# Attention with a routed feed-forward: values loaded once and repeated on GpSimd, and products grouped by the columns they use

## Chip, core and metric

The kernel runs on one core of a Trainium2 chip. The metric is device time in microseconds (us). The core has five engines: TensorE (PE, with its weight loads shown as PEld), VectorE (DVE), ScalarE (ACT), GpSimd (POOL) and SyncE (SP, which issues most transfers). Each executes its own instructions in the order in which the program lists them; an instruction that waits holds everything behind it on its engine.

## The reference

Eight batches of eight heads, 576 positions, 64 numbers a head. Four heads attend to the last 32 positions, four to every fourth of the last 128 (the "dilated" heads). The result, 4608 rows of 512, goes through a mixture of experts: noisy gating picks two of eight experts for each row.

```python
scores = scale * np.matmul(q, k.transpose(0, 1, 3, 2))
mask_plain = (rel >= 0) & (rel < window)                                        # window 32
mask_dil = (rel >= 0) & (rel < window * dilation) & (rel % dilation == 0)       # dilation 4
attn = softmax(scores where masked)
x = (attn @ v) as rows of 512
noisy_logits = x @ w_gate + log1p(exp(x @ w_noise)) * noise
for e in range(E):                                                              # top two experts of a row
    h = np.maximum(x[mask] @ w1[e], 0.0)
    out[mask] += top2_w[mask, k, None] * (h @ w2[e])
```

## The kernel before, in words

**Attention** works through 8 groups of 3 steps. Group g holds two batches and one kind of head: even groups the dilated heads, odd groups the plain ones. K and Q of a kind stand in one buffer (`KT`, `QT`), V of the dilated heads in `VD`, of the plain heads in two tiles `VP`. Loads for later groups are entered in a table of slots (`at(slot, f)`), two slots a step, and are issued by SP when the program comes to the slot.

A step is: mask products (`identb` times a mask, all 128 output columns), 24 score products that use 32 columns each (`qk`), a maximum and a subtraction on DVE, an exponential on ACT (`expo`), six 128-column transposes of the result (`ptr`), copies to SBUF on ACT, 24 value products of 32 columns (`pv`), and a division on DVE. The result `x` of an older step is stored to DRAM, transposed (`x_transpose`, 128 columns), and multiplied with the gating weights (`gate_mm`, 32 columns); `gate_front` transposes three pieces of the logits in half of the steps. Step i of the loop issues, in this order, the scores of step i, the transposes of step i-1, the slot's fillers, the transposes of x of step i-2, the exponential of step i, the values of step i-1 and the gating product of step i-2.

In one value product the 128 rows of V are 64 own positions and the 64 before and between them: for a block of 64 positions, the windows need three pieces of 32 positions, and the middle one twice. The array `vdl` (`vpl`) in DRAM holds 128 rows of such windows, so that each position is loaded twice. V has a second axis `w`; rows of the other `w` are zero and are cleared once at the start, on ACT for `VD`, on DVE and POOL for `VP`.

**Setup**: POOL and DVE build masks and constants. `setup_a`, `setup_b` and `setup_c` are fillers of the slots 2, 4 and 5. `setup_b` writes an index table `tokc` on POOL and computes on it on DVE; `setup_c` prepares rows of padding, some of it in slots 6, 12 and 18.

**Gating and routing** (`gate`) runs in small pieces between the attention steps (`micro`). Its scatters to the table `tab` are indirect DMAs on POOL; a copy from the newest `x` to a one-element tile `spacer` holds POOL back so that only some of them are issued in a step. The first expert's rows are gathered by indirect DMAs on POOL as well.

**Experts**: eight experts, three blocks of rows each, products `up` and `dn` on TensorE, which is in order, so that the first of them stands behind the last piece of attention.

Of the kernel before, what the change touches and what calls it, by code (L numbers as in the profile page):

```python
# [9 lines left out]
F32 = mybir.dt.float32  # L10
# [15 lines left out]
U = 4  # L26
# [14 lines left out]
US_W2 = 3.0, 3.5  # L41
LAG = 15
US_X = (17, 52)


@with_exitstack
def attention_moe_kernel(ctx, tc, qt, kp, kd, vpl, vdl, w_gate, w_noise, noise, w1, w2, out, CAPS=(1216, 1216, 1216, 1184, 1184, 1152, 1152, 1152), SPLITS=(0, 384, 896)):
# [65 lines left out]
    def v_loads(g):  # L113
        u, ty = g // 2, 1 - g % 2
        if ty:
            d = VD.rearrange("p w j h y c -> p w (j h y c)")
            n = d.shape[2] // 3
            for i in range(3):
                for w in range(2):
                    yield lambda i=i, w=w: sync.dma_start(d[w:128:2, w, n * i:n * i + n],  # L120
                                                          vdl[u, w:128:2, n * i:n * i + n])
        else:
            for b in range(2):
                for w in range(2):
                    yield lambda b=b, w=w: sync.dma_start(VP[b][w:128:2, w].rearrange("p j h c -> p (j h c)"),
                                                          vpl[u, b, w:128:2])
# [7 lines left out]
    gpsimd.memset(KT[1][:, 1], 0.0)  # L134
    for f in qk_loads(0, 2):
        f()

    def clear_by_copy(t):
        scalar.copy(t, none.to_broadcast(list(t.shape)) if len(t.shape) == 2 else
                    none.unsqueeze(2).unsqueeze(3).to_broadcast(list(t.shape)))  # L140

    VF = VD.rearrange("p w j h y c -> p w (j h y c)")
    for w in range(2):
        clear_by_copy(VF[:, w])
    clear_by_copy(KT[0][:, 0])


# [45 lines left out]
            p0 = 64 * x + 32 * h  # L193
            gpsimd.tensor_copy(m[p0:p0 + 32, 6 * h], m0[p0:p0 + 32, 1])
    vector.memset(KT[0][:, 1], 0.0)
    for b, w, eng in ((0, 0, vector), (0, 1, gpsimd), (1, 0, gpsimd), (1, 1, gpsimd)):
        eng.memset(VP[b][:, w], 0.0)
# [153 lines left out]

    SB, PE_, PT, XG, XT, GS = {}, {}, {}, {}, {}, {}

    def qk(k):
        g, st = divmod(k, 3)
        ty = 1 - g % 2
        s = aps.tile([128, 8, 2, 64], F32, name="s", tag="s")
        for e in (0, 4):
            n = min(4, 6 - e)
            tensor.matmul(s[:, e:e + n], lhsT=identb,  # L360
                          rhs=masks[ty][:, 6 * st + e:6 * st + e + n].unsqueeze(2).to_broadcast([128, n, 2, 64]),
                          start=True, stop=False, skip_group_check=True)
        for e in range(6):
            for qd in range(4):
                if ty == 0:
                    x = qd // 2
                    b, ub = divmod(12 * st + 6 * (qd % 2) + e, 18)
                else:
                    x = qd
                    b, ub = divmod(6 * st + e, 9)  # L370
                tensor.matmul(s[32 * qd:32 * qd + 32, e], lhsT=QV[ty][:, b, x, 32 * ub:32 * ub + 32],  # L371
                              rhs=KV[ty][:, :, b, x, 32 * ub:32 * ub + 64],
                              start=False, stop=True, skip_group_check=True)
        a = sm.tile([128, 2, 6, 64], F32, name="a", bufs=1)
        mx = sm.tile([128, 6, 2], F32, name="mx")
        vector.tensor_reduce(mx, s[:, 0:6], axis=AX.X, op=OP.max)
        vector.tensor_tensor(a.rearrange("p y e c -> p e y c"), s[:, 0:6], mx.unsqueeze(3).to_broadcast([128, 6, 2, 64]), op=OP.subtract)
        SB[k] = a

    def expo(k):  # L380
        p = sm.tile([128, 6, 64, 2], F32, name="pe")
        scalar.activation(p.rearrange("p j c w -> p j w c"), SB.pop(k).rearrange("p y (j w) c -> p (y j) w c", w=2),
                          AF.Exp, scale=0.125)
        PE_[k] = p

# [14 lines left out]
    def pv(k):  # L400
# [510 lines left out]
    def at(kb, *fs):  # L911
        fill.setdefault(kb, []).extend(fs)
# [3 lines left out]
    for g in range(2 * U):  # L916
        s0 = 6 * g
        if g + 1 < 2 * U:
            for i, f in enumerate(v_loads(g + 1)):
                at(s0 + 3 + 2 * (i // 2), f)  # L920
# [3 lines left out]
    fronts = {6 * u + 6 + st: (u, st) for u in range(U) for st in range(3)}  # L924
    def idx_late(before, a, b, then):
        while any(g in gens for g in before):
            yield 1
# [36 lines left out]
    for t0, n, kb in ((0, 9, 17), (9, 9, 29), (18, 6, 39), (24, 3, 41), (27, 6, 51)):  # L964
        at(kb, lambda t0=t0, n=n: gens.append(gate(t0, n)))
    L0 = 12 * (U - 1)
    at(29, lambda: (new_idx(0), gens.append(idx_late(list(gens), 0, SPLITS[1], lambda: x_block(0)))))
    at(41, lambda: gens.append(idx_late(list(gens), SPLITS[1], SPLITS[2], lambda: x_block(1))))
    at(2, setup_a)
    at(4, setup_b)  # L970
    at(5, setup_c)
    for f in v_loads(0):
        f()
    for f in qk_loads(1):
        f()

# [31 lines left out]
    for i in range(NS + 2):  # L1008
        slot[0] = 2 * i
        early[0] = True  # L1010
        micro(2)
        early[0] = False
        if i < NS:
            qk(i)
        micro(2)
        if i >= 2:
            move_x(i - 2)
        micro(2)
        if 1 <= i <= NS:
            ptr(i - 1)  # L1020
        micro(2)
        micro(2)
# [7 lines left out]
        micro(2)  # L1030
        if 1 <= i <= NS:
            pv(i - 1)
        micro(2)
# [8 lines left out]
    for f in fronts.values():  # L1042
        gate_front(*f)
    gens.append(gate(33, 3))

# [137 lines left out]
def _layouts(q, k, v):  # L1183
# [10 lines left out]
    def windows(a):  # L1194

        n = a.shape[1] // 64
        a = np.pad(a, ((0, 0), (32, 0)) + ((0, 0),) * (a.ndim - 2))
        p = np.arange(128)[:, None]
        at = 64 * np.arange(n) + p // 2 + 32 * (p % 2)
        return a[:, at]  # L1200

    qt = np.stack([heads(q, ty).reshape(U, 128, 4 * S) for ty in range(2)], 1)
    pad = ((0, 0),) * 4 + ((32, 0),)
# [2 lines left out]
    def with_ones(a):  # L1206
        return np.concatenate([a, np.ones(a.shape[:-1] + (1,), np.float32)], -1)

    vpl = windows(with_ones(v[:, 0:4].transpose(0, 2, 1, 3))).reshape(U, 2, 128, -1)

    dil = v[:, 4:8].reshape(U, 2, 4, S // 4, 2, 2, D).transpose(0, 1, 4, 3, 2, 5, 6).reshape(U, S, 4, 2, D)
    vdl = windows(with_ones(dil)).reshape(U, 128, -1)
    return {"qt": qt, "kp": kp, "kd": kd, "vpl": vpl, "vdl": vdl}


# [18 lines left out]
```

## Time and profile before

| | |
|---|---|
| median of 3 runs | 1081.24 us (1080.13 to 1085.15) |
| span of the profiled execution | 1086.8 us |
| granted TensorE clock, mean | 0.963 |
| PE busy | 1011.7 us (93%) |
| PEld / DVE / ACT / POOL busy | 79% / 43% / 29% / 49% |
| first mask product, step 0 | 9.6 us |
| first mask product, step 23 | 197.6 us |
| first expert product | 227.2 us |

The profiled execution is 5.6 us longer than the median, and 1.7 us longer than the longest run. A row of the timeline gives the start, the time, engine and line, output and inputs, and in brackets how long the engine had been idle and what ended that. A busy PE is not a PE at its peak. PE is above 97% busy from 400 us to the end, so that the first 227 us, where the change lies, are to be read apart from the whole.

### The profile page before, as it was taken

The page shows a single profiled execution, that of the slowest core. Times are in us where ns is not written, and L with a number is a line of the kernel's source. Part 1 is how long each engine was busy: PE and PEld are TensorE (multiplying, and loading weights), DVE is VectorE, ACT ScalarE, POOL GpSimd, SP SyncE. Part 2 cuts the span into 40 slices and gives each one's busy share as a digit, 9 for nine tenths or more (in the row PEclk, how much of TensorE's full clock was granted, in tenths as well). Part 3 has the DMA queues.
Part 4 walks back from the last instruction along what each step waited for, and adds up shares of the span by engine and source line. Part 5 has one row for each costly group of instructions (what it writes and reads, how often), then busy time and mean ns, then how long its engine had stood idle before and what let it go on. Part 6 is the DMA issues. An engine that isn't in the chain of part 4 may idle for free. (4 is left out here: it accounts for less than half of the span.)

```text
span 1086.8 us, 18768 instructions
## 1 busy us (share of the span) xinstructions
PE 1011.7 (93%) x7274; PEld 855.7 (79%) x7275; DVE 465.7 (43%) x1060; ACT 319.4 (29%) x609; POOL 534.5 (49%) x727
## 2 busy tenths in 40 slices
PE   6896877778989999999999999999999999999996
PEld 4774655567878989988997889788978888888885
DVE  7673635635225444344434352435353434343221
ACT  6673534622113322222223131312131222222110
POOL 7004243455776655755644564466455645553112
PEclk9998887878999999999999999999999999999999
DMA  8898687455255243533533352426242623453123
GB/s 280 313 315 278 194 283 257 151 164 186 43 96 129 54 109 85 109 84 86 91 85 85 86 131 50 102 64 135 38 112 52 137 39 108 75 119 72 24 28 45
DMA packets 79214, 132.95 MB, mean 122 GB/s; under 512 B 31648, under 2 KB 41296, under 8 KB 77840
## 3 DMA queue, kind: packets, MB, share of 16 engines
q1 hardware_dynamic: 56768, 92.56, 27.6%
q0 software_dynamic: 22352, 39.15, 19.6%
q8 instruction: 58, 0.95, 0.4%
q14 instruction: 36, 0.29, 0.1%
HBM read 92.11 MB, written 39.54 MB: 121 GB/s over the span
## 5 line engine op out<-in xcount | busy, mean ns | idle before, releaser
L826 PE MATMUL up<-x,w1h 128*128 128x512 f32 (+4 forms) x1536 | 396.7, 344 | 10.9 <-issue 8.2
L778 POOL DMA_INDIRECT g<-xs,ixi x258 | 269.7, 1045 | 84.0 <-issue 78.6
L826 PEld LDWEIGHTS up<-x,w1h 128*128 128x128 f32 x1536 | 273.1, 189 | 37.2 <-issue 8.7
L826 PE MATMUL up<-x,w1l 128*128 128x384 f32 (+4 forms) x768 | 263.4, 343 | 0.0
L868 PE MATMUL dn<-w2h,hh 128*128 128x512 f32 x576 | 225.5, 392 | 0.0
L868 PE MATMUL dn<-w2l,hh 128*128 128x512 f32 x576 | 224.7, 390 | 0.0
L868 PE MATMUL dn<-w2h,hl 128*128 128x512 f32 x576 | 224.6, 390 | 0.0
L832 DVE SCALAR_TENSOR_TENSOR hl<-up,hh 128x384 fp32r<-128x384 f32 (+2 forms) x192 | 106.7, 557 | 249.1 <-ACT hh L830 187.0
L830 ACT ACTIVATE hh<-up 128x384 fp32r<-128x384 f32 (+4 forms) x192 | 94.6, 498 | 298.7 <-PE up L826 248.7
L845 POOL DMA_INDIRECT out_rows<-y,ixs x67 | 107.3, 1602 | 141.4 <-DVE y L877 119.0
L826 PEld LDWEIGHTS up<-x,w1l 128*128 128x128 f32 x768 | 145.4, 189 | 11.8
L877 DVE TENSOR_SCALAR y<-dn,ixs 128x512 f32<-128x512 f32 x63 | 47.3, 751 | 188.2 <-PE dn L868 163.5
L868 PEld LDWEIGHTS dn<-w2h,hl 128*128 128x128 f32 x576 | 108.4, 188 | 22.7
L868 PEld LDWEIGHTS dn<-w2h,hh 128*128 128x128 f32 x576 | 108.5, 188 | 22.0
L868 PEld LDWEIGHTS dn<-w2l,hh 128*128 128x128 f32 x576 | 108.5, 188 | 21.8
L797 ACT CAST x<-xr 128x512 fp32r<-128x512 f32 x67 | 40.5, 605 | 216.0 <-DVE xr L795 175.8
L306 POOL COPY spacer<-hh 1x1 f32<-1x1 f32 x72 | 26.4, 366 | 131.9 <-ACT hh L830 131.6
L628 POOL DMA_INDIRECT tab<-en,si x72 | 71.8, 998 | 36.1 <-issue 16.2
L798 DVE TENSOR_TENSOR x<-xr,x 128x512 fp32r<-128x512 f32 x67 | 44.7, 667 | 17.9 <-ACT x L797 12.4
L371 PE MATMUL s<-kt,qt 128*32 128x128 f32 x1152 | 41.2, 288 | 9.9 <-DMA qt<-in_qt 5.4
L371 PEld LDWEIGHTS s<-kt,qt 128*32 128x32 f32 x1152 | 32.5, 115 | 20.3 <-issue 19.6
L708 DVE TENSOR_TENSOR w1l<-ws,w1h 128x1024 fp32r<-128x1024 f32 x32 | 38.8, 1218 | 20.8 <-ACT w1h L706 10.9
(186 smaller groups left out, 867.2 us busy)
## 6 DMA issues: line engine op xcount, KB each, us to landing
ws<-in_moe_w SPq DMA_DIRECT2D x36, 512.0 KB
ws<-in_moe_w SPq DMA_DIRECT2D x112, 128.0 KB
out_rows<-zero SPq DMA_DIRECT2D x38, 256.0 KB
vd<-in_vdl SPq DMA_DIRECT2D x24, 390.0 KB
vp<-in_vpl SPq DMA_DIRECT2D x16, 585.0 KB
qt<-in_qt SPq DMA_DIRECT2D x14, 576.0 KB
xs<-x SPq DMA_DIRECT2D x24, 256.0 KB
kt<-in_kd SPq DMA_DIRECT2D x16, 320.0 KB
```

Source lines behind the costliest of these rows:

```text
L371: tensor.matmul(s[32 * qd:32 * qd + 32, e], lhsT=QV[ty][:, b, x, 32 * ub:32 * ub + 32], rhs=KV[ty][:, :, b, x, 32 * ub:32 * ub + 64], star ...
L628: ins = gpsimd.indirect_dma_start(out=tab, out_offset=bass.IndirectOffsetOnAxis(ap=si[:, kq, t:t + 1], axis=0), in_=en[:, kq, t], in_offse ...
L708: return lambda: vector.tensor_tensor(b, s, a.bitcast(F32), op=OP.subtract)
L778: gpsimd.indirect_dma_start(out=g[:, j], out_offset=None, in_=xq, in_offset=bass.IndirectOffsetOnAxis(ap=IX[e][1][:, r0 // 32 + j:r0 // 32 ...
L797: scalar.copy(xh[:, :, o:o + rn], xr[:, :, 0:rn])
L798: return lambda: vector.tensor_tensor(xl[:, :, o:o + rn], xr[:, :, 0:rn], xh[:, :, o:o + rn].bitcast(F32), op=OP.subtract)
L826: tensor.matmul(p[:, 0:n], lhsT=a[:, 128 * f:128 * f + 128], rhs=b[:, kc, 0:n], start=(i == 0), stop=(i == 11))
L830: scalar.activation(hh[:, f, 0:n], p[:, 0:n], AF.Relu)
L832: vector.scalar_tensor_tensor(hl[:, f, 0:m], p[:, 0:m], 0.0, hh[:, f, 0:m].bitcast(F32), op0=OP.max, op1=OP.subtract)
L845: ins = gpsimd.indirect_dma_start(out=out, out_offset=bass.IndirectOffsetOnAxis(ap=sc[0:rn, t, 1:2], axis=0), in_=y[0:rn], in_offset=None, ...
L868: tensor.matmul(p[0:rn], lhsT=a[:, f, o:o + rn], rhs=b[:, f % 2], start=(i == 0), stop=(i == 23))
L877: vector.tensor_scalar(y[0:rn], p[0:rn], wsc, None, op0=OP.mult)
```

## The change

Two things are changed.

First, V is loaded once. DRAM holds blocks of 64 rows instead of 128; `v_load` loads 32 rows for each `w` (rows 32 to 63 for w = 0, rows 96 to 127 for w = 1), and `v_repeat` makes the other two pieces: rows 64 to 95 of w = 1 are a copy of rows 32 to 63 on POOL, rows 0 to 31 of w = 0 (which are the block before) a copy of rows 96 to 127 on POOL for the groups 0 to 3, and one more load for the groups 4 to 7 (`VCOPY = 4`). Only the quarters that stay zero are cleared. `VP[1]` is cleared in slot 3, behind `setup_a`.

Second, the order in a step: 128-column products first (x transposes of step i-3, the logits' transposes, mask products, transposes of step i-1), then those of 32 columns (scores of step i, gating of step i-3, values of step i-1), then the exponential. In `pv` the last two rows of each head come behind the first four of all heads, in an order in which neighbours use different columns. The gate's slots move by one.

```diff
+VCOPY = 4
-                    yield lambda i=i, w=w: sync.dma_start(d[w:128:2, w, n * i:n * i + n],
-                                                          vdl[u, w:128:2, n * i:n * i + n])
...
+    def v_load(g, i):
+        b, j0, j1 = v_parts(g)[i]
+        n = VB[1 - g % 2]
+        for w in range(2):
+            sync.dma_start(VF[1 - g % 2][b][32 + 64 * w:64 + 64 * w, w, n * j0:n * j1],
+                           v_source(g, b)[32 * w:32 * w + 32, n * j0:n * j1])
+    def v_repeat(g, i, w):
+        b, j0, j1 = v_parts(g)[i]
+        n, t = VB[1 - g % 2], VF[1 - g % 2][b]
+        if w:
+            gpsimd.tensor_copy(t[64:96, 1, n * j0:n * j1], t[32:64, 0, n * j0:n * j1])
+            return
+        j0 = max(j0, 1)
+        dst, src = t[0:32, 0, n * j0:n * j1], (n * (j0 - 1), n * (j1 - 1))
+        if g < VCOPY:
+            gpsimd.tensor_copy(dst, t[96:128, 1, src[0]:src[1]])
+        else:
+            sync.dma_start(dst, v_source(g, b)[32:64, src[0]:src[1]])
...
-    for b, w, eng in ((0, 0, vector), (0, 1, gpsimd), (1, 0, gpsimd), (1, 1, gpsimd)):
-        eng.memset(VP[b][:, w], 0.0)
+    for i in range(3):
+        v_repeat(0, i, 1)
+        v_repeat(0, i, 0)
+    def clear_plain(b):
+        for w, eng in ((1, (vector, gpsimd)[b]), (0, gpsimd)):
+            eng.memset(VF[0][b][64 - 64 * w:128 - 64 * w, w], 0.0)
+        gpsimd.memset(VF[0][b][0:32, 0, 0:VB[0]], 0.0)
+    clear_plain(0)
...
-        for hh in range(4):
-            for r, a, jp, b, ub in blocks(st, ty):
+        bl = list(blocks(st, ty))
+        for hh, rows in [(hh, bl[0:4]) for hh in range(4)] + [(hh, bl[4:6]) for hh in (0, 2, 1, 3)]:
...
     at(2, setup_a)
+    at(3, lambda: clear_plain(1))
     at(4, setup_b)
...
+        if 3 <= i < NS:
+            x_transpose(i - 3)
+        micro(2)
+        for f in fronts.pop(i, []):
+            gate_front(*f)
         if i < NS:
-            qk(i)
+            mask_scores(i)
+        micro(2)
+        if 1 <= i <= NS:
+            ptr(i - 1)
         micro(2)
         if i >= 2:
             move_x(i - 2)
         micro(2)
-        if 1 <= i <= NS:
-            ptr(i - 1)
         fillers(2 * i)
         if i >= 2:
             store_x(i - 2)
-            x_transpose(i - 2)
         if i < NS:
-            expo(i)
+            qk(i)
         micro(2)
+        if 3 <= i < NS:
+            gate_mm(i - 3)
         if 1 <= i <= NS:
             pv(i - 1)
-        if i >= 2:
-            if i in fronts:
-                gate_front(*fronts.pop(i))
-            gate_mm(i - 2)
+        if i < NS:
+            expo(i)
```

POOL at the start, from the last mask piece to the table `tokc`. Before (vp is `VP`, wg the gating weights, zero and tokc tiles of the setup):

```order
L194 CAST mask_143<-m_129 32x64 x4
L197 MEMSET vp_94 128x2340
L197 MEMSET vp_95 128x2340 x2
L212 MEMSET wg 128x128
...
L227 MEMSET zero 128x512
L232 MEMSET tokc 128x144
L233 IOTA tokc 128x36
```

and in the changed kernel:

```order
L136 COPY vd<-vd 32x1560
L141 COPY vd<-vd 32x1040
L136 COPY vd<-vd 32x1560
L141 COPY vd<-vd 32x1560
L136 COPY vd<-vd 32x1560
L141 COPY vd<-vd 32x1560
L218 MEMSET vp_94 64x2340
L219 MEMSET vp_94 32x260
L236 MEMSET wg 128x128
...
L218 MEMSET vp_95 64x2340 x2
L219 MEMSET vp_95 32x260
...
L257 IOTA tokc 128x36
```

Six copies stand ahead of setup_a, and three clears between setup_a and the write of tokc, where three clears stood ahead of setup_a.

DVE around setup_b, whose first and last row here are the ones on tokc. Before (mx and a are the maximum and difference of a step's scores, den and x its division):

```order
L376 TENSOR_REDUCE mx<-s 128x12
L377 TENSOR_TENSOR a<-s,mx 128x6x2x64
L237 TENSOR_SCALAR tc_380<-tokc 128x36
...
L261 COPY tokc<-tc_378 128x36 x2
L421 TENSOR_SCALAR den<-o 128x6 x2
```

and in the changed kernel:

```order
L458 TENSOR_TENSOR x<-o,den 128x384 x2
L261 TENSOR_SCALAR tc_361<-tokc 128x36
...
L285 COPY tokc<-tc_359 128x36 x2
L407 TENSOR_REDUCE mx<-s 128x12
L408 TENSOR_TENSOR a<-s,mx 128x6x2x64
```

The rows on tokc stood behind the maximum and the difference of step 2, and now stand ahead of them, behind the division of step 0.

PE in one step of a group (step 6 before; pp takes the transposes and the gating products, xtp the transposes of x, o the values):

```order
L360 MATMUL s<-mask_144,identb 128x512
L360 LDWEIGHTS identb
L360 MATMUL s<-mask_144,identb 128x256
L371 MATMUL s<-kt_98,qt_100 32x128 x24
L396 MATMUL pp_194<-ident,pe 128x128 x4
L396 MATMUL pp_195<-ident,pe 128x128 x2
L449 MATMUL xtp<-ident,x 128x128 x6
L414 MATMUL o<-vp_95,pt 32x130 x24
```

and in the changed kernel:

```order
L481 MATMUL xtp<-ident,x 128x128 x6
L386 LDWEIGHTS identb
L386 MATMUL s<-mask_151,identb 128x512
L386 LDWEIGHTS identb
L386 MATMUL s<-mask_151,identb 128x256
L427 MATMUL pp_206<-ident,pe 128x128 x4
L427 MATMUL pp_207<-ident,pe 128x128 x2
L402 MATMUL s<-kt_98,qt_100 32x128 x24
L503 MATMUL pp_207<-xt,wg 32x128 x4
L503 MATMUL pp_207<-xt,wg 32x64 x4
L446 MATMUL o<-vp_95,pt 32x130 x24
```

The scores stood ahead of the transposes `pp<-pe` of the step before them, and now stand behind these.

More of the change, by code (lines that the diff above doesn't have):

```diff
@@ L136, in attention_moe_kernel @@
         f()
+    for i in range(3):
+        v_load(0, i)
     def clear_by_copy(t):
[L139 to L144, printed above, removed]
+        scalar.copy(t, none[0:t.shape[0]].to_broadcast(list(t.shape)))
+    clear_by_copy(VF[1][0][0:64, 1])
+    clear_by_copy(VF[1][0][64:128, 0])
+    clear_by_copy(VF[1][0][0:32, 0, 0:VB[1]])
     clear_by_copy(KT[0][:, 0])
@@ L195, in attention_moe_kernel @@
     vector.memset(KT[0][:, 1], 0.0)
-    for b, w, eng in ((0, 0, vector), (0, 1, gpsimd), (1, 0, gpsimd), (1, 1, gpsimd)):
-        eng.memset(VP[b][:, w], 0.0)
+    for i in range(3):
+        v_repeat(0, i, 1)
[5 more added lines that the diff above has]
+    clear_plain(0)
     tri = consts.tile([128, 128], BF, name="tri")
@@ L362, in qk @@
                           start=True, stop=False, skip_group_check=True)
+    def qk(k):
+        g, st = divmod(k, 3)
+        ty = 1 - g % 2
+        s = SC.pop(k)
         for e in range(6):
@@ L404, in pv @@
         o = aps.tile([128, 2, 512], F32, name="o", tag="o")
-        for hh in range(4):
-            for r, a, jp, b, ub in blocks(st, ty):
+        bl = list(blocks(st, ty))
+        for hh, rows in [(hh, bl[0:4]) for hh in range(4)] + [(hh, bl[4:6]) for hh in (0, 2, 1, 3)]:
+            for r, a, jp, b, ub in rows:
                 qd, c0 = (r, hh) if r < 4 else (2 * (r - 4) + hh // 2, 4 + hh % 2)
@@ L918, in attention_moe_kernel @@
         if g + 1 < 2 * U:
-            for i, f in enumerate(v_loads(g + 1)):
-                at(s0 + 3 + 2 * (i // 2), f)
+            for i in range(len(v_parts(g + 1))):
+                s1 = s0 + 3 + 2 * i
+                at(s1, lambda g=g, i=i: v_load(g + 1, i))
+                for w in (1, 0):
+                    at(s1 + (3 if w or g + 1 < VCOPY else 0), lambda g=g, i=i, w=w: v_repeat(g + 1, i, w))
         if g + 2 < 2 * U:
@@ L923, in attention_moe_kernel @@
                 at(s0 + 7 + 2 * (i // 3), f)
-    fronts = {6 * u + 6 + st: (u, st) for u in range(U) for st in range(3)}
+    fronts = {6 * u + 7 + st: [(u, st)] for u in range(U - 1) for st in range(3)}
+    fronts[6 * U + 1] = [(U - 1, 0), (U - 1, 1)]
+    fronts[6 * U + 2] = [(U - 1, 2)]
     def idx_late(before, a, b, then):
@@ L1025, in attention_moe_kernel @@
             store_x(i - 2)
-            x_transpose(i - 2)
+        if i < NS:
+            qk(i)
+        micro(2)
+        if 3 <= i < NS:
+            gate_mm(i - 3)
+        if 1 <= i <= NS:
+            pv(i - 1)
         if i < NS:
             expo(i)
[L1030 to L1033, printed above, removed]
-        if i >= 2:
-            if i in fronts:
-                gate_front(*fronts.pop(i))
-            gate_mm(i - 2)
+        for k in {NS: (NS - 3, NS - 2), NS + 1: (NS - 1,)}.get(i, ()):
+            micro(2)
+            x_transpose(k)
+            gate_mm(k)
         micro(2)
@@ L1041, in attention_moe_kernel @@
     early[0] = True
-    for f in fronts.values():
+    for f in sum(fronts.values(), []):
         gate_front(*f)
@@ L1192, in heads, with blocks @@
         return a.transpose(0, 6, 5, 1, 2, 4, 3).reshape(U, 128, 2, 4, S // 2)
[L1194 to L1200, printed above, removed]
+    def blocks(a):
+        n, s = a.shape[0], a.shape[1]
+        a = a.reshape((n, s // 64, 2, 32) + a.shape[2:])
+        return np.moveaxis(a, 1, 3)
     qt = np.stack([heads(q, ty).reshape(U, 128, 4 * S) for ty in range(2)], 1)
@@ L1207, in with_ones @@
         return np.concatenate([a, np.ones(a.shape[:-1] + (1,), np.float32)], -1)
-    vpl = windows(with_ones(v[:, 0:4].transpose(0, 2, 1, 3))).reshape(U, 2, 128, -1)
+    vpl = blocks(with_ones(v[:, 0:4].transpose(0, 2, 1, 3))).reshape(U, 2, 64, -1)
     dil = v[:, 4:8].reshape(U, 2, 4, S // 4, 2, 2, D).transpose(0, 1, 4, 3, 2, 5, 6).reshape(U, S, 4, 2, D)
-    vdl = windows(with_ones(dil)).reshape(U, 128, -1)
+    vdl = blocks(with_ones(dil)).reshape(U, 64, -1)
     return {"qt": qt, "kp": kp, "kd": kd, "vpl": vpl, "vdl": vdl}
```

36 lines of the change are left out of this document (14 added, 22 removed).

## The prediction, made before the changed kernel ran

> **What bounds the kernel now.** I read the windows first, then the timeline of one undisturbed attention step, then the start, then the stretches where PE stood still. In the windows the columns are the stretch, its length, busy time of PE, PEld, DVE, ACT and POOL, the granted clock, the DMA share and GB/s.
>
> ```profile
> span 1086.8 us, 18768 instructions
> ```
>
> ```profile
> 10.00:20.00 10.00, 6.09 (x153) 4.73 (x153) 6.40 (x6) 5.08 (x6) 9.62 (x8) 1.00 1.01 413
> 400.00:1087.00 687.00, 674.66 (x3376) 583.45 (x3374) 262.97 (x417) 155.81 (x261) 347.70 (x424) 1.00 0.39 81
> ```
>
> ```profile
> 83.44:227.24 143.80, 104.98 (x1674) 77.74 (x1671) 68.45 (x253) 64.11 (x157) 55.11 (x98) 0.81 0.69 220
> 36.52:83.44 46.92, 45.86 (x1031) 37.85 (x1028) 33.82 (x115) 34.81 (x88) 0.85 (x2) 1.00 0.93 317
> ```
>
> Three stages differ. From 400 us on PE is busy 98% of the time in the experts: nothing there is touched, so whatever attention gains or loses up to the first expert product reaches the end. Steps 4 to 11 (36.52 to 83.44) keep PE busy 98% at full clock, with DMA at 93%: 5.87 us a step, set by PE, not by data. From 83.44 PE is busy 73% at a clock of 0.81. The start is the fourth stage, below.
>
> One step of stage two, with the next one's first product, and two starts of steps that contain the logits' transposes:
>
> ```profile
> 36.52 0.50 PE L360 MATMUL s<-mask,identb 128*128 128x512 bf16 x2
> 36.95 1.52 PE L371 MATMUL s<-kt,qt 128*32 128x128 f32 x48
> 38.40 0.87 PE L396 MATMUL pp<-ident,pe 128*128 128x128 f32 x6
> 38.56 0.96 DVE L376 TENSOR_REDUCE mx<-s 128x12 f32<-128x768 f32 x1 [0.70 <-PE s L371]
> 39.11 0.82 PE L449 MATMUL xtp<-ident,x 128*128 128x128 f32 x6
> 39.85 1.56 PE L414 MATMUL o<-vp,pt 128*32 128x130 f32 x44
> 41.90 0.50 PE L360 MATMUL s<-mask,identb 128*128 128x512 bf16 x2
> ```
>
> ```profile
> 110.93 0.50 PE L360 MATMUL s<-mask,identb 128*128 128x512 bf16 x2
> 116.93 0.50 PE L360 MATMUL s<-mask,identb 128*128 128x512 bf16 x2
> ```
>
> So a step costs 5.38 us, or 6.00 with the logits' transposes, and PE passes from piece to piece without waiting.
>
> **The change part by part.**
>
> *The order of a step.* PE changes between 128 and 32 columns four times in a step before (six with the logits), twice now. The scores need 1.45 us for 48 passes, the 48 value and 16 gating passes 2.05 us; at the scores' rate (0.030 us a pass) these would need 1.93. A change costs at most what the 0.82 us of six x transposes exceed five sixths of their 0.74 (39.11 to 39.85), 0.2 us. With two or four changes less, PE's own work falls to about 4.9 us (5.38 - 0.12 - 0.4) or 5.1. But PE is not what then decides. Ahead, the scores of step i+1 were issued before the transposes of step i; now they stand behind them, and these need the exponential of step i. The shortest passages of that chain:
>
> ```profile
> 13.01 0.96 DVE L376 TENSOR_REDUCE mx<-s 128x12 f32<-128x768 f32 x1
> 14.00 0.96 DVE L377 TENSOR_TENSOR a<-s,mx 128x768 f32<-128x768 f32 x1
> 14.99 0.95 ACT L382 ACTIVATE pe<-a 128x768 f32<-128x768 f32 x1 [2.65 <-DVE a L377]
> 33.39 0.86 ACT L397 COPY pt<-pp 128x512 f32<-128x512 f32 x2 [2.40 <-PE pp L396]
> 34.47 1.57 PE L414 MATMUL o<-vd,pt 128*32 128x130 f32 x44
> ```
>
> Start of scores to start of maximum 38.56 - 36.95 = 1.61; maximum to end of exponential 15.94 - 13.01 = 2.93; from ACT's end to PE 34.47 - 34.25 = 0.22; six transposes 39.11 - 38.40 = 0.71, then scores again: 5.47 us. PE's other pieces (gating, values, x transposes, logits, masks) fit beside DVE and ACT. A step thus costs 5.5 us, now with or without the logits, against a mean of 5.7. Steps 4 to 11: 46.9 - 8 x 5.5, a gain of 2.9. Of the 12 later steps about half run undisturbed: 6 x 0.2, a gain of 1.2.
>
> *Loads.* Two rows on the issues of V, with count and size, and one on PE.
>
> ```profile
> vd<-in_vdl SPq DMA_DIRECT2D x24, 390.0 KB
> vp<-in_vpl SPq DMA_DIRECT2D x16, 585.0 KB
> ```
>
> ```profile
> 88.38 1.32 PE L371 MATMUL s<-kt,qt 128*32 128x128 f32 x18 [3.44 <-issue]
> ```
>
> 18.7 MB fall by half for four groups and by a quarter for four, by about 7 MB, 22 us at 317 GB/s. Since no step behind the third waits for data, that is hidden. What it can free is PE's stop ahead of 88.38, which no other engine ends and which lies right behind the stretch with full transfers: I count its 3.4 us as gained.
>
> *The start.* Here the change lengthens a queue that is waited for.
>
> ```profile
> 9.94 0.23 POOL L194 CAST mask<-m 32x64 bf16<-32x64 f32 x1
> 10.23 6.02 POOL L197 MEMSET vp<- 128x2340 f32 x3
> 11.44 1.52 PE L371 MATMUL s<-kt,qt 128*32 128x128 f32 x48 [1.39 <-DMA qt<-in_qt]
> 16.20 0.19 POOL L212 MEMSET wg<- 128x128 f32 x1
> 21.81 0.53 POOL L227 MEMSET zero<- 128x512 f32 x1
> 22.56 0.27 POOL L233 IOTA tokc<- 128x36 int32 x1
> 23.95 0.28 DVE L237 TENSOR_SCALAR tc<-tokc 128x36 int32<-128x36 int32 x1
> 28.39 0.29 DVE L261 COPY tokc<-tc 128x36 int32<-128x36 int32 x2
> 29.95 2.31 PE L371 MATMUL s<-kt,qt 128*32 128x128 f32 x48 [4.05 <-DMA qt<-in_qt]
> 32.18 1.54 PE L396 MATMUL pp<-ident,pe 128*128 128x128 f32 x6
> ```
>
> ```profile
> L190 POOL CAST mask<-m 128x1152 bf16<-128x1152 f32 x1 | 1.2, 1195 | 0.1
> ```
>
> Before, POOL cleared V for 6.0 us, ran setup_a from 16.20 to 22.34, and wrote tokc by 22.83; DVE used it at 23.95 without having waited. Now: the first V piece (0.39 MB) lands behind qt, which released PE at 11.44; at 413 GB/s that is 0.95 us later, about 12.5. Then six copies of 1560 or 1040 numbers, 8840 in all. No copy of that kind is in the trace; the nearest row converts 1152 numbers in 1195 ns, 1.04 ns each, so 9 us. From below the price is nothing; from above I take double, 18. Then one clear and a small one (2.3, by 6.02 / 3), setup_a (6.1), two clears and a small one (4.3), and 0.5 for tokc: 12.5 + 9 + 2.3 + 6.1 + 4.3 + 0.5 = 34.7. The DVE rows on tokc, 4.7 us, end at 39.4. Queued behind them on DVE is the maximum of step 2, whose scores are done long before; behind it stand the mask products of step 3, which need the buffer s, and with them all of PE. Maximum and difference of step 2 end at 41.4, the exponential at 42.4; transposes and scores of step 3 at the cold clock (1.54 and 2.31 above) end near 46.3; step 4's maximum comes 5.5 and a few tenths later, at 52.2, against 38.56 before. The start loses 13.6 us, although the wait of 4.05 us for qt is gone. With copies for nothing it would lose 4.6, with 18 us 22.6.
>
> [...]
>
> *Later copies and the tail.* Each later part is loaded 1.5 steps ahead of its copies; groups 1 to 3 meet an idle POOL (busy 0.85 us in 36.52 to 83.44). Two of them stand ahead of a clear of padding that DVE waits for: 1 us. From group 4 the copies stand among the scatters:
>
> ```profile
> 197.62 0.48 PE L360 MATMUL s<-mask,identb 128*128 128x512 bf16 x2
> 227.24 0.99 PE L826 MATMUL up<-x,w1h 128*128 128x384 f32 x2
> ```
>
> ```profile
> 142.94 0.97 POOL L628 DMA_INDIRECT tab<-en,si  x1 [0.51 <-issue]
> 151.84 0.96 POOL L628 DMA_INDIRECT tab<-en,si  x1 [0.23 <-issue]
> ```
>
> ```profile
> 154.79 0.23 DVE L421 TENSOR_SCALAR den<-o 128x6 f32<-128x6 f32 x2 [9.92 <-PE gt L509]
> ```
>
> During and just after the run of eight scatters from 142.94 to 152.80, DVE had nothing for 9.92 us and PE issued one product at a time. About as many scatters fall into attention afterwards, so I keep those stalls. At the end the x transposes and gating of one more step (0.7 + 0.5, and copies between them) stand between step 23 and the first expert product: 2 us.
>
> **Sum**, against the profiled execution's span: 13.6 - 2.9 - 1.2 - 3.4 + 1 + 2 = 9.1 us. The median lies 5.6 us under that span, and I carry the difference over: 1081.2 + 9 = 1090 us.
>
> **Rivals.**
>
> *The scatters' stalls shrink* (faster). Stage three needs 143.8 us where 12 steps of 5.7 and a tail as long as two more would take 80. If the stalls come from scatters meeting full transfers, at a DMA share of 0.69, then 7 MB less, and copies that break runs of eight scatters into fours, may take half of the 64 us: 1090 - 32 = 1058; a quarter gives 1074. I take 1070, nearer to the quarter, since PE stands still beside a busy POOL with transfers at 0.41 too:
>
> ```profile
> 236.00:246.00 10.00, 4.05 (x24) 3.73 (x22) 2.18 (x7) 0.32 (x2) 8.12 (x15) 0.81 0.41 103
> ```
>
> *The start costs little* (no change). If copies run far above the converting row's rate, the loss is 4.6, and the sum 0.1: 1081.
>
> *Copies late among scatters* (slower still). From group 4 the first value product of a group needs a copy that queues behind up to eight scatters, 10 us; where that comes last, 4 us for each of four groups: 1106.
>
> **Chances and range.** The forecast 0.50, stalls shrink 0.25, cheap start 0.14, late copies 0.11. About 0.5% (5.4 us) can be told from no change. Faster takes nearly all of the first rival and a little of the second, 0.25; within 0.5%, most of the second and the forecast's lower edge, 0.20; slower 0.55. The forecast's own range is 1085 to 1099, from copies at half to one and a half times the price taken. To hold 8 in 10 the range reaches 1067 to 1104, which leaves out a tenth on each side.
>
> **What will show it.** Right: DVE idle until about 35 us ahead of its first row on tokc, waiting for POOL; step 4's mask product near 49 us instead of 36.52; steps 5 to 11 of even length near 5.5, the transposes `pp` released by ACT's exponential; first expert product near 236. Wrong: DVE reaching tokc before 28; steps below 5.2 us, which would mean that the chain is shorter than its rows; stage three below 125 us; PE released by POOL copies at the first value product of groups 4 to 7.

## Result and profile after

The changed kernel takes 1131.5 us (median of 4 runs, 1128.6 to 1133.6), the kernel before 1080.7 beside it: 1.0463 times as long, 95% interval 1.043 to 1.0497. The forecast was 1090. The profiled executions differ by 41.5 us (1086.8 and 1128.3); the span of before lies 6.1 us over that median, that of the change 3.2 under its own, which makes the 50.8.

The kernel before takes 1081 to 1084 us in some sessions and 1026 to 1029 in others, so every ratio below is to runs of the kernel before in the same session. Expected times that start from 1081 us belong to the first kind, and are to be read as differences.

The windows of the changed kernel, cut at the same events as in the prediction: start, steps 4 to 11, step 12 to the first expert product, the rest.

```profile
span 1128.3 us, 18823 instructions
10.00:20.00 10.00, 7.44 (x131) 5.54 (x132) 4.62 (x5) 4.78 (x6) 3.56 (x4) 0.83 1.03 291
60.11:121.78 61.67, 46.37 (x1029) 38.38 (x1027) 37.11 (x110) 35.75 (x90) 17.47 (x12) 0.92 0.72 223
121.78:266.92 145.14, 103.12 (x1688) 77.77 (x1686) 71.98 (x260) 65.07 (x158) 67.96 (x100) 0.84 0.63 188
266.92:1128.30 861.38, 836.90 (x4154) 721.63 (x4152) 336.93 (x610) 198.97 (x336) 463.57 (x591) 0.99 0.41 88
```

Step 4 starts at 60.11 instead of 36.52: the start lost 23.6 us. Steps 4 to 11 take 61.67 instead of 46.92: 14.8 more, with the same PE work (46.37 and 45.86 busy). Step 12 to the first expert product takes 145.1 instead of 143.8, the rest 1.8 more. So 38 of the 41 us are gone before step 12. And in the first row the transfers are as busy as before (share 1.03 and 1.01) but move 291 GB/s instead of 413.

The start, from the timeline:

```profile
16.51 1.48 POOL L136 COPY vd<-vd 32x1560 f32<-32x1560 f32 x1 [6.33 <-DMA vd<-in_vdl]
38.49 0.27 POOL L257 IOTA tokc<- 128x36 int32 x1
38.80 0.20 DVE L261 TENSOR_SCALAR tc<-tokc 128x36 int32<-128x36 int32 x1 [15.57 <-POOL tokc L257]
39.81 2.17 POOL L136 COPY vp<-vp 32x2340 f32<-32x2340 f32 x1
39.82 0.17 DVE L269 SCALAR_TENSOR_TENSOR tc<-tc,tc 128x9 int32<-128x9 int32 x1
39.92 2.10 DVE L268 TENSOR_SCALAR tc<-tokc 128x9 int32<-128x9 int32 x1
42.04 1.92 POOL L141 COPY vp<-vp 32x2080 f32<-32x2080 f32 x1
42.05 1.93 DVE L269 SCALAR_TENSOR_TENSOR tc<-tc,tc 128x9 int32<-128x9 int32 x1
51.32 0.29 DVE L285 COPY tokc<-tc 128x36 int32<-128x36 int32 x2
53.57 0.82 PE L386 MATMUL s<-mask,identb 128*128 128x512 bf16 x2 [26.39 <-DVE a L408]
```

POOL waits for V until 16.51, and reaches `tokc` at 38.49; DVE has waited 15.57 us for it. Then DVE's rows on `tokc` need 12.8 us (38.80 to 51.6) instead of 4.7: a row over 9 numbers takes 0.17 us, such rows 1.93 or 2.10 when they start beside a POOL copy (the one at 39.82, which starts with its copy, 0.17), and they end when that copy does (39.92 + 2.10 and 39.81 + 2.17). PE stands still for 26.39 us.

Step 4 after that, up to the mask product of step 5:

```profile
60.11 0.49 PE L386 MATMUL s<-mask,identb 128*128 128x512 bf16 x2
60.82 0.88 PE L427 MATMUL pp<-ident,pe 128*128 128x128 f32 x6 [0.23 <-ACT pe L413]
63.24 0.96 DVE L407 TENSOR_REDUCE mx<-s 128x12 f32<-128x768 f32 x1 [1.89 <-PE s L402]
65.45 0.49 PE L386 MATMUL s<-mask,identb 128*128 128x512 bf16 x2
```

It lasts 5.34 us, and the transposes `pp` are released by ACT's exponential, as forecast.

Step 6:

```profile
75.49 1.48 POOL L136 COPY vd<-vd 32x1560 f32<-32x1560 f32 x1 [26.96 <-DMA vd<-in_vdl]
78.03 0.41 POOL L305 MEMSET free<- 128x388 int32 x1
78.47 0.26 DVE L306 COPY free<-free 128x194 int32<-128x194 int32 x1 [6.42 <-POOL free L305]
78.65 1.53 DVE L307 TENSOR_SCALAR free<-free 128x97 int32<-128x97 int32 x1
80.06 0.94 DVE L407 TENSOR_REDUCE mx<-s 128x12 f32<-128x768 f32 x1
80.13 1.48 POOL L141 COPY vd<-vd 32x1560 f32<-32x1560 f32 x1
82.10 0.84 ACT L413 ACTIVATE pe<-a 128x768 f32<-128x768 f32 x1 [5.77 <-DVE a L408]
83.50 0.90 PE L541 MATMUL gt<-ident,gs 128*128 128x128 f32 x3 [5.71 <-ACT xt L483]
```

POOL's queue holds a copy that waits for its data, behind it the clear of padding, on which DVE waits 6.42 us, and behind that DVE's maximum. SP issued the load of that data from 66.7 us on, and it landed at 75.4. The step takes 13.28 us. The same happens in step 9 (9.39 us, DVE waits 4.53).

### The profile page after: what moved, and what is told of

It is laid out like the page before. It is cut to its first block, busy times and chain, and to the rows that moved or that the text cites. A ratio compares the mean times of both kernels' runs of the same rounds, so it can differ in the third digit from the quotient of the medians.

```text
span 1128.3 us, 18823 instructions
## 1 busy us (share of the span) xinstructions
PE 1012.4 (90%) x7274; PEld 855.5 (76%) x7275; DVE 480.2 (43%) x1060; ACT 320.8 (28%) x610; POOL 585.9 (52%) x759
## 3 DMA queue, kind: packets, MB, share of 16 engines
q1 hardware_dynamic: 55968, 85.10, 26.3%
## 5 line engine op out<-in xcount | busy, mean ns | idle before, releaser
L136 POOL COPY vd<-vd 32x1560 f32<-32x1560 f32 x12 | 17.9, 1490 | 76.5 <-DMA vd<-in_vdl 52.2
L402 PE MATMUL s<-kt,qt 128*32 128x128 f32 x1152 | 43.8, 292 | 3.7 <-issue 3.4
```

## Experiments

Step and product are starts in us; the ratio is to the kernel before of the same session.

| kernel | ratio (95%) | step 4 | step 12 | first expert product |
|---|---|---|---|---|
| before, result's session | 1 | 36.5 | 83.4 | 227.2 |
| change, result's session | 1.0463 | 60.1 | 121.8 | 266.9 |
| before, a 1029 us session | 1 | 36.2 | 83.5 | 191.7 |
| change, same session | 1.0754 (1.0716 to 1.0793) | 61.2 | 122.9 | 257.1 |

**The order alone**: the second part of the change, with V loaded twice in the old layout.

```diff
+    def mask_scores(k):
...
+        if 3 <= i < NS:
+            x_transpose(i - 3)
```

> The new order of a step alone, with V loaded twice as before. Theory A (the loss sits in POOL's queue: copies that wait for V's data, and what DVE waits for behind them): nothing of it is here, steps without logits stay near 5.4 us, those with logits take 6.5 instead of 6.0 because their transposes now wait for ACT's copies xt; the mask products of step 4 start near 37 us; the time is 1079 to 1090. Theory B (the order itself costs: scores behind the exponential and behind the transposes): 1110 or more, with steps 6 to 11 as long as in the changed kernel (mean 8.6 us).

Measured 1036.4 us, 1.0084 (1.0056 to 1.0113); step 4 at 38.1, step 12 at 87.5, first expert product at 191.5. As theory A has it. The order gains nothing, and 5 us of its loss lie behind the first expert product (845.4 us from there to the end, 840.2 before, in two sessions), which I did not follow.

**The copies alone**: the first part, with the old order.

```diff
+    def v_load(g, i):
...
+    def v_repeat(g, i, w):
```

> V loaded once and repeated by copies on POOL, with the order of a step as before the change. Theory A: step 4's mask product starts near 58 to 60 us instead of 36.5, DVE waits again for POOL's clear of padding once in step 6 and once in step 9 (about 6 and 4.5 us), and the time is 1081 + 23 + 11 = 1115, at least 1105. Theory B: under 1095, since only the order costs. If both parts are needed together (the order leaves PE less slack for what POOL makes late), this run and the one with the order alone add up to clearly less than the 50 us of the whole.

Measured 1097.4 us, 1.0666 (1.0618 to 1.0714); step 4 at 57.7, first expert product at 259.3. Theory B falls. Theory A's start is there, but the loss is 71 us and not its 34: behind step 12 PE waits 30.6 us for copies of V, on which neither theory had counted (the prediction's third rival had, with 16). DVE's two waits for the padding, 11.6 us, fall in steps 7 and 10, not 6 and 9. The order's 0.8% and the copies' 6.7% add up to the 7.5% of the whole change in such a session, so the parts do not need each other.

**Padding cleared on DVE.**

```diff
-            gpsimd.memset(padt, 0)
+            vector.memset(padt, 0)
```

> The changed kernel with the three clears of padding (128 x 388 int32) on DVE instead of POOL, so that DVE no longer waits there for POOL's queue; nothing else moves. Theory A: the waits of 6.42 and 4.53 us ahead of DVE's rows on the padding are gone and nothing takes their place, steps 6 and 9 take 6.5 and 5.5 us (13.28 and 9.39 in the changed kernel), and the time falls by 10 to 11 us, to about 1120. Rival: the copies are as late as before and the value products that need them wait instead; the time stays within 3 us of 1131.

Measured 1.0649 (1.06 to 1.0698) against the change's 1.0754: 10.8 us less. Steps 6 and 9 take 6.85 and 5.42 us. Something does take their place: steps 10 and 11 grow from 7.73 and 6.79 us (change, 1029 us session) to 9.31 and 8.38, which is open. A wait of DVE on one short POOL row, queued behind copies, was worth 1%.

**Group 0's repeats by DMA.**

```diff
+VDMA = (0,)
-        if w:
+        if w and g not in VDMA:
             gpsimd.tensor_copy(t[64:96, 1, n * j0:n * j1], t[32:64, 0, n * j0:n * j1])
             return
+        if w:
+            sync.dma_start(t[64:96, 1, n * j0:n * j1], v_source(g, b)[0:32, n * j0:n * j1])
+            return
...
-        if g < VCOPY:
+        if g < VCOPY and g not in VDMA:
```

> The changed kernel with the repeated rows of group 0's V brought by DMA from HBM instead of copied on POOL (as many bytes for this group as before the change); all other groups are copied as in the changed kernel. Theory A (POOL stands at the start waiting for V and then copies, until 25.3 us): POOL reaches tokc near 24 us instead of 38.8, DVE's rows on it are done before 32, step 4's mask product starts near 40 instead of 60, and the time falls by about 20 us to 1111. Rival C (it is not the wait but DVE's rows being stretched beside POOL copies, 12.8 us instead of 4.7): they still meet the copies of group 1, step 4 starts near 48, and the time falls by 12.

Measured 1.0637 (1.0592 to 1.0682): 12 us less. POOL writes `tokc` at 23.4, DVE's rows end at 32.4, as theory A has it; but step 4 starts at 46.9, because the next thing in POOL's queue becomes the wait: copies of group 1, whose V lands only at 38.

```profile
38.08 2.13 POOL L137 COPY vp<-vp 32x2340 f32<-32x2340 f32 x1 [13.43 <-DMA vp<-in_vpl]
42.58 0.26 DVE L310 COPY free<-free 128x194 int32<-128x194 int32 x1 [5.40 <-POOL free L309]
42.76 2.18 DVE L311 TENSOR_SCALAR free<-free 128x97 int32<-128x97 int32 x1
```

So 12 us fit rival C's figure for another reason than C's.

**The kernel before, and the change, in one session**, both unaltered.

> The kernel before, profiled on the chip of this study, for the experiments beside it. The chip of the prediction's profile gave 1081 us and stops of PE beside the scatters (143.8 us from step 12 to the first expert product); the chip of the experiments gave 1026 us. Theory A: attention's first twelve steps and the experts last as long on both, and the 55 us lie in the twelve later steps, which here take about 90 us and show hardly any stop of PE that ends by nothing but its own issue. Rival: the clock is lower or the experts slower, and the 55 us are spread over the whole span.

> The changed kernel unaltered, on the same chip. If the 12 later steps lose nothing by the change here either, as in the two profiles of the prediction's chip, it costs the same 50 us: 1026 + 50 = 1076. If the copies of groups 4 to 7 queue behind scatters and that shows once PE is not stopped by other things (the run with group 0 by DMA had 32 us of PE released by copies behind step 12), it costs about 80 us: 1105.

Measured 1033.7 and 1107.5 us. Of the 55 us between the two profiles of the kernel before, 36 lie from step 12 to the first expert product: 108.2 us here (first row), 143.8 in the prediction's profile, with the same work and a granted clock of 0.92 instead of 0.81. The other 19 lie behind it (840.2 us to the end, and 859.6), so that theory A, which had all 55 in the twelve later steps and 90 us for them, holds in part. The expectations put the difference down to the chip; no run shows that. The change takes 134.2 there (second row), and 1107.5 us in all is the second case of its expectation.

```profile
83.50:191.72 108.22, 88.59 (x1673) 69.46 (x1671) 68.45 (x253) 64.32 (x157) 56.50 (x98) 0.92 0.91 290
```

```profile
122.89:257.07 134.18, 86.29 (x1688) 70.62 (x1686) 74.80 (x260) 64.82 (x158) 68.56 (x100) 0.85 0.68 202
```

The change costs 25.0 us up to step 4, 14.4 in steps 4 to 11, 26.0 in steps 12 and later, 8.3 behind. The first two are those of the result's session (23.6, 14.8); the third is extra, and the fourth was 1.8 there. There PE waits for the copies, and a copy for scatters (waits on PE from 120 to 260 us, then the timeline):

```profile
PE o L446 <- POOL vd L136: 18.5, 4, 5.9
PE o L446 <- POOL vp L136: 17.3, 3, 10.4
```

```profile
134.80 0.97 POOL L660 DMA_INDIRECT tab<-en,si  x1 [0.22 <-issue]
141.77 1.48 POOL L136 COPY vd<-vd 32x1560 f32<-32x1560 f32 x1 [6.00 <-DMA tab<-en,si]
```

POOL was free at 135.8, and this part of V had landed by 126.3, yet the copy starts at 141.8, when the last scatter has landed. The program says why; this is the wait list of that copy, DMASW being the scatters' completions:

```
74 L136 COPY vd<-vd 32x1560 [waits DMASW5_49,DMASW6_49,DMASW4_49,DMAHW3_49,DMASW3_49,PE_49]
```

**Repeats of groups 4 to 7 by DMA**, with the same edit and another list; the loads of these rows stand in the slots of the other loads of V.

```diff
+VDMA = (4, 5, 6, 7)
```

> The changed kernel with all repeated rows of groups 4 to 7 brought by DMA (as many bytes for these groups as before the change), so that no copy is among the scatters; groups 0 to 3 as in the changed kernel. Theory D (late copies): PE is no longer released by copies behind step 12, the scatters run in longer runs, and the time falls by about 30 us against the changed kernel of this call. Rival: the scatters and gathers stop PE just as long without the copies, as they did in both profiles of the prediction's chip; it falls by less than 8.

Measured 1.0528 (1.0474 to 1.0581): 23 us less than the change. PE waits for no copy there, and step 12 to the first expert product takes 112.5 us. Theory D, with 23 of its 30 us.

**All repeats by DMA.**

```diff
+VDMA = (0, 1, 2, 3, 4, 5, 6, 7)
```

> The changed kernel with every repeated row brought by DMA and no copy of V on POOL: the new layout and the new order stay. If POOL's copies are the whole loss, this is as the order alone: within 1% of the kernel before (1026 to 1037 where that takes 1026), step 4 near 38 us, steps with logits 6.5. If the new layout or the smaller transfers (32 rows each) cost something of their own, it is 1045 or more.

Measured 1067 us, 1.0369 (1.0329 to 1.041), the second case: without any copy, as many bytes as before, and still 2.9% above the order alone. Of the 25 us that it has lost to the order alone by the first expert product, 7 lie before step 4 and 16 behind step 12. Windows from 40 to 80 us of the order alone, and of this run:

```profile
40.00:80.00 40.00, 35.52 (x871) 30.34 (x860) 25.77 (x68) 28.00 (x71) 0.42 (x1) 1.00 0.94 325
```

```profile
40.00:80.00 40.00, 35.17 (x825) 30.59 (x821) 22.39 (x50) 25.65 (x64) 0.85 (x2) 0.95 0.97 283
```

The transfers are as busy and move 13% less. In the packet records V's rows of 6240 bytes take 238 ns (median) with the order alone and 395 here.

**Small transfers into spread rows**, with the order alone.

```diff
-                    yield lambda i=i, w=w: sync.dma_start(d[w:128:2, w, n * i:n * i + n],
-                                                          vdl[u, w:128:2, n * i:n * i + n])
+                    for r in (w, w + 2):
+                        yield lambda i=i, w=w, r=r: sync.dma_start(d[r:128:4, w, n * i:n * i + n],
+                                                                   vdl[u, r:128:4, n * i:n * i + n])
...
```

> The new order alone, V loaded twice in the old layout, but each of V's transfers split into two of 32 rows, every fourth row of the 128: as many and as small transfers as in the run in which all repeats came by DMA (1.0369 of the kernel before, against 1.0084 with the order alone). Theory P (a transfer into 32 adjacent rows of SBUF, or two such, is slow: packets of 6240 bytes took 391 to 404 ns there and 238 where rows are spread over all 128): spread rows are fast however small the transfer, 280 to 320 GB/s from 40 to 120 us, 1.005 to 1.012 of the kernel before. Rival N (the number of transfers, of which eight can be under way, sets it): 1.03 or more, 260 to 285 GB/s.

Measured 1.0054 (1.0029 to 1.0079), 308 GB/s from 40 to 80 us and 291 from 80 to 120, packets of V at 238 ns again. The ratio is of a 1084 us session and does not compare with 1.0369; the packets do. Theory P: here the rows that a transfer fills set its speed, not its size. The rows read in DRAM changed with those filled in SBUF, but Q, loaded from 128 adjacent rows into 128 adjacent rows, takes 178 ns for 4608 bytes in every one of these runs, as fast for its size as 238 for 6240, so that adjacent rows in DRAM were not slow of themselves here.

**Group 1's repeats by DMA.**

```diff
+VDMA = (1,)
```

> The changed kernel with the repeated rows of group 1's V alone brought by DMA, so that no POOL copy runs beside DVE's rows on tokc (in the changed kernel single int32 rows of DVE take 1.9 to 2.1 us instead of 0.17 to 0.43 while a POOL copy of 32 x 2340 or 2080 runs). Theory C (while POOL copies, a DVE row that works from SBUF to SBUF stands still until the copy is over): no row of DVE on tokc takes over 0.5 us, they take 4.7 us together instead of 12.8, step 3's mask product starts near 45 instead of 53.2, and the time falls by about 8 us, from 1.0754 to about 1.068 of the kernel before. Rival (the rows are slow because they wait for iotas or for one another): 12 us again, and no change of the time.

Measured 1.0365 (1.0301 to 1.0429) against 1.0463: 10.6 us less, step 3 at 46.4 instead of 53.6. DVE's rows on `tokc` take 5.2 us (39.17 to 44.4), none over 0.42. Theory C.

**The logits behind the values**, with the order alone.

```diff
-    def pv(k):
+    def pv(k, front=()):
...
+        for f in front:
+            gate_front(*f)
         ov = o[:, :, 0:390].rearrange("p b (c w d) -> p w b c d", c=3, w=2)
```

> The new order with V loaded as before, and the logits' transposes put behind the value products (DVE's reduction of them ahead of the value products' divisions). With the order alone the nine steps with logits of the first three batches take 6.5 us, PE waiting for ACT's copies xt. Theory: that wait goes, these steps take 6.0, which is what PE's own pieces need, and the time falls by 4 to 5 us, from 1.0084 to about 1.004 of the kernel before; steps without logits stay at 5.4, so the order gains nothing over the old one at best. If the chain through DVE and ACT decides these steps too, they take 6.5 again.

Measured 1.0041 (1.0011 to 1.0071); the spread-row run, the same order in that session, gave 1.0054. Steps 6 to 8, those with logits, take 7.24, 5.56 and 7.09 us, and 7.11, 6.54 and 6.55 there: PE waits 1.0 us in all for ACT's copies, yet these steps are hardly shorter, and the two ratios cannot be told apart. My expectation fails; what sets them now is open.

**POOL's setup ahead of the copies**, with the padding cleared on DVE. `setup_b2` is DVE's part of `setup_b`.

```diff
-    for i in range(3):
-        v_repeat(0, i, 1)
-        v_repeat(0, i, 0)
...
     at(2, setup_a)
+    at(2, setup_b)
+    for i in range(3):
+        for w in (1, 0):
+            at(2, lambda i=i, w=w: v_repeat(0, i, w))
     at(3, lambda: clear_plain(1))
-    at(4, setup_b)
...
+        at(4, lambda: setup_b2(t, v, s, i0, z, a))
```

> The changed kernel with the pads cleared on DVE (as in the run that gave 1.0649 of the kernel before) and POOL's setup work up to tokc put ahead of group 0's copies in POOL's queue; every copy is still made. Theory A (at the start not the copies' length but what stands behind them in POOL's queue costs): POOL writes tokc near 20 us instead of 38.5, DVE's rows on it are done before 30, step 4's mask product starts near 40 instead of 60, and the time falls by about 20 us against 1.0649, to 1.045. Rival (the copies themselves are what PE waits for, since V comes late): the value products of steps 0 to 3 wait for POOL instead, step 4 starts after 50, and less than 10 us are gained.

Measured 1.0297 (1.024 to 1.0354), 18 us under the change of such a session. POOL writes `tokc` at 19 us, but step 4 starts at 54.2: theory A's wait is gone and only 6 us are gained at the start, because rows that stand still beside POOL take its place. DVE's rows run from 26.63 to 44.3, 17.7 us:

```profile
28.54 4.12 POOL L214 MEMSET vp<- 64x2340 f32 x2
28.68 1.94 DVE L269 TENSOR_SCALAR tc<-tokc 128x9 int32<-128x9 int32 x1
30.64 0.17 DVE L270 SCALAR_TENSOR_TENSOR tc<-tc,tc 128x9 int32<-128x9 int32 x1
30.75 1.94 DVE L269 TENSOR_SCALAR tc<-tokc 128x9 int32<-128x9 int32 x1
33.60 2.09 DVE L269 TENSOR_SCALAR tc<-tokc 128x9 int32<-128x9 int32 x1
```

Beside this POOL clear, which only writes, the rows with one input take 1.94 us and the row with two inputs 0.17 (also in the run with group 1 by DMA: 0.17 us at 40.19, under a clear until 40.51); beside copies both kinds stand still (2.09 us at 33.60 and 1.93 at 35.73).

**Copies of groups 0 and 1 on ACT**, on top of the last.

```diff
-            gpsimd.tensor_copy(dst, t[96:128, 1, src[0]:src[1]])
+            (scalar.copy if g < 2 else gpsimd.tensor_copy)(dst, t[96:128, 1, src[0]:src[1]])
...
```

> As the run with POOL's setup work ahead of the copies and the pads cleared on DVE (step 4's mask product at 54.2 us, DVE's rows on tokc from 26.6 to 44.3), with the copies of groups 0 and 1 on ACT instead of POOL. Theory C (DVE's rows stand still while POOL copies or clears in SBUF): with no POOL copy beside them these rows take under 6 us again, the clear of V still locking a few, step 4 starts near 43, and the time falls by about 11 us. Rival: it is the late V that counts, ACT's exponentials now wait behind copies that wait for V, and step 4 starts after 50 as before.

Measured 1.0535 (1.047 to 1.06), 11.7 us under the run with the padding on DVE. The rows on `tokc` take 5.5 us, step 4 starts at 39.25, step 5 at 50.19 instead of 59.17:

```profile
17.70 1.49 ACT L136 COPY vd<-vd 32x1560 f32<-32x1560 f32 x1
24.23 0.48 DVE L269 TENSOR_SCALAR tc<-tokc 128x9 int32<-128x9 int32 x1
24.84 0.16 DVE L269 TENSOR_SCALAR tc<-tokc 128x9 int32<-128x9 int32 x1
28.55 0.29 DVE L286 COPY tokc<-tc 128x36 int32<-128x36 int32 x2
```

The same copies are as long on ACT (1.49 us) as on POOL (1.48), and no row on `tokc` beside them takes over 0.55. The rival has a part: ACT's copies for group 1 then hold its exponentials, and step 4 lasts 10.9 us.

**POOL copies beside DVE's rows by themselves**, in the kernel before.

```diff
+    extra = acon.tile([64, 1088], BF, name="extra")
...
+        for _ in range(8):
+            gpsimd.tensor_copy(extra[0:32], extra[32:64])
```

> The kernel before with eight copies on POOL (32 x 1088 bf16, about 1 us each, to a tile that nothing reads) put behind POOL's iotas, so that they run beside DVE's rows on tokc, which take 4.6 us there (25.2 to 29.8). Theory C: single rows of DVE stretch to the length of a copy, their sum grows to 10 us or more, the maximum behind them comes 5 us later, and the time grows by 3 to 5 us (part of the delay lies beside the wait for qt). Rival (POOL's copies leave DVE alone, and the rows were slow for another reason): 4.6 us, and no row over 0.5.

Measured 1.0063 (1.0034 to 1.0093), 6.6 us, over the 3 to 5 expected; step 4 at 43.6 instead of 36.2. The rows take 11.7 us (25.07 to 36.8) instead of 4.6. The maximum, whose input is in PSUM, was not held: in step 6 above it takes 0.94 us beside a copy, and in the changed kernel the one at 19.75 us, which starts under a copy that runs from 19.16 to 20.65, takes 0.96.

```profile
25.05 9.27 POOL L281 COPY extra<-extra 32x1088 bf16<-32x1088 bf16 x8
25.07 1.12 DVE L237 TENSOR_SCALAR tc<-tokc 128x36 int32<-128x36 int32 x1
26.33 1.00 DVE L239 SCALAR_TENSOR_TENSOR tc<-tc,tc 128x36 int32<-128x36 int32 x1
36.47 0.29 DVE L261 COPY tokc<-tc 128x36 int32<-128x36 int32 x2
```

**All repairs together**: the copies on ACT, and

```diff
+VDMA = (4, 5, 6, 7)
```

> The changed kernel with everything repaired that the runs named: pads cleared on DVE, POOL's setup work ahead, copies of groups 0 and 1 on ACT, repeated rows of groups 4 to 7 by DMA; copies on POOL remain for groups 2 and 3 only. If the account closes, what is left is the new order (1.004 to 1.008 of the kernel before), the slower transfers of V, and what the copies on ACT take: 1.015 to 1.03. If something large is missing from the account, it stays above 1.035.

Measured 1.0296 (1.0236 to 1.0356), the upper edge of the expected range. Taken one after the other, the repairs divide the 7.5% of a 1029 us session: padding 1.05%, POOL's queue and the rows that stand still at the start 1.14% (padding on DVE to copies on ACT), late copies 2.39% (copies on ACT to this run), and 2.96% left. They add up by construction; what the run shows is the size of the rest. The order explains 0.84% of these; for the other 2.1% the slower transfers (2.85% where all repeats came by DMA) and ACT's copies are at hand, neither divided nor shown to fill it. No version here beats the kernel before.

## Why the prediction was wrong

The direction and the bound (all that attention loses up to the first expert product reaches the end) were right: 39.7 us are lost there, 41.5 at the end. The sizes were not: 9.1 us were forecast. Two steps failed. DVE's rows were priced as if POOL's copies beside them cost nothing, and POOL's copies later on by their length, without the wait for their data. In their place the runs show rows on `tokc` that are held for 8.1 us, and 10.8 us behind two clears of padding. V's first landing was also put 4.0 us too early.

*The start, forecast 13.6 us.* Measured 24.7 from maximum to maximum of step 4 (38.56 and 63.24). POOL's copies (8.8 us, 9 forecast) and what follows them up to `tokc` (13.5, 13.2 forecast) were right. The term "V lands 12.5" was 4.0 short, for two reasons. It put V right behind the qt that released PE at 11.44. But SP issues the second halves of K and Q between the two, in the kernel before too (SPq is an issue by SP):

```profile
5.61 1.11 SPq L108 DMA_DIRECT2D kt<-in_kd  x2
6.76 0.58 SPq L111 DMA_DIRECT2D qt<-in_qt  x1
7.39 3.97 SPq L120 DMA_DIRECT2D vd<-in_vdl  x3
```

There the first 390 KB of V land at 15.3, 2.8 us later than the term. The other 1.2 go with the slower transfers: V had been priced at 413 GB/s, the old layout's rate, and in the changed kernel 291 were moved from 10 to 20 us. The term "DVE rows on tokc, 4.7 us" was 8.1 short: they were priced as they stood, without asking what POOL does beside them. From the end of these rows to the maximum of step 4 it took 11.6 instead of 12.8; the clock that the forecast calls cold there was granted at 0.62 and 0.50 in the kernel before (29.95 to 32.18 and 32.18 to 33.80), and at 0.50 and 0.57 in the changed kernel (53.57 to 55.00 and 55.00 to 57.00). 13.6 + 4.0 + 8.1 - 1.2 = 24.5.

*Steps 4 to 11, forecast -2.9.* Measured +14.8. The chain of 5.5 us was right for steps 4 and 5 (5.34 and 5.47). "Now with or without the logits" failed: those steps take 6.5, because the logits' transposes were given a place right behind the x transposes and need ACT's copies of these (PE waits 1.04 us for them at the end of step 8, which takes 6.5). "Two of them stand ahead of a clear of padding that DVE waits for: 1 us" is the large miss: the copies were priced by their length, not by their wait for data in an in-order queue. It was 6.42 and 4.53 us of waiting, and two rows held for 1.5 and 2.2 us; the run with the padding on DVE gives 10.8. The order alone takes 49.4 us for these steps, 5.4 over the forecast of 8 x 5.5; the two together nearly make the 17.7 us that the change took over it.

*Loads.* "About 7 MB less, hidden" was true, but there was no relief in it:

```profile
q1 hardware_dynamic: 56768, 92.56, 27.6%
```

```profile
q1 hardware_dynamic: 55968, 85.10, 26.3%
```

27.6% of 1086.8 us and 26.3% of 1128.3 are 300 and 297 us of the 16 engines: 8% fewer bytes, 1% less time.

*Late copies, rival with 0.11.* It came true in the session of 1029 us, with 26 us instead of 16, and by a wait for the scatters' landing rather than for their turn in the queue. In the result's session PE waits 6.6 us for a copy once, and from step 12 to the first expert product it takes as long as before. That this is near the forecast (2.6 less) is luck: up to the start of step 23 it is 7.6 us shorter, where 4.6 had been forecast, and behind that 8.9 longer instead of 2, with the 6.6 among them. In that session the kernel before takes 36 us more in the same place than in the other, and how the change's waits lie beside that is not shown. The two other rivals fell: step 12 to the first expert product did not get shorter, and the copies were not cheap (1480 ns for 1560 numbers, 0.95 each, against 1.04 in the forecast).

*Signs.* DVE idle up to 38.8 us waiting for POOL and step 4 near 60 instead of 49 point to the right mechanism and the wrong size. The even steps near 5.5 failed (5.34 to 13.28). PE released by copies at the first value products was listed as a sign of error, and is what the later session shows.

## What to carry to other kernels

Before work is moved to an engine with a queue of its own, list everything that stands behind it there and who waits for that: a row that waits for data costs those behind it the wait, not its length (in step 6 DVE waited 6.42 us for a clear behind a copy of 1.48). Price a DVE row of the kinds that stood still here (`tensor_scalar` in SBUF, or two inputs from SBUF) that starts beside a POOL copy at what is left of the copy, as in these runs (1.93 to 2.10 us for 0.17). Before bytes saved are counted as time, ask whether the new transfer still fills rows all over SBUF: here 8% fewer bytes took 1% less time, with packets of 6240 bytes at 359 ns (median, changed kernel) instead of 238.

## What the runs showed of the hardware

*DVE stands still beside POOL.* Rows of 0.17 us take 1.9 to 2.1 beside copies of 1.9 to 2.2, 1.0 to 1.1 beside copies of about 1.1, and 0.48 at most when ACT makes the copies. A row that starts within 0.01 us of its copy came out both ways: 1.93 at 35.73 in the run with POOL's setup ahead, 0.17 at 39.82 in the change. In the change the maximum from PSUM was not held (0.96 us at 19.75), nor a reciprocal from SBUF (0.23 us at 218.66, under a copy from 217.01 to 219.14). Beside the clear only the rows with one input stood still (1.94 and 0.17 us). What holds the rows is not shown. I had not asked this of the change.

*Transfers into 32 adjacent rows were slow.* Packets of 6240 bytes take 238 ns (median) into every second or every fourth row, 395 into 32 adjacent ones where all repeats came by DMA, and 359 in the changed kernel; those of 9360 bytes take 353 in the kernel before and 575 in the changed one. What slows them is not shown.

*The sessions.* In some the kernel before loses 36 us more from step 12 on, beside its scatters, PE issuing one product at a time with no other engine to wait for, and 19 us more behind the first expert product. Nothing run here tells why.
